# ReLU²-attention followed by an h-swish MLP: the MLP begins at step 30 instead of 33, and the splits of x move with it

## Chip, cores and metric

One Trainium2 chip (trn2), one core. The metric is the device time of one launch in microseconds (us), the median over the runs of a kernel. The engines are PE (TensorE), DVE (VectorE), ACT (ScalarE), POOL (GpSimd) and SP (SyncE, which here only issues DMAs; its queue of issues is written SPq).

## What is computed

```python
scores = (1.0 / S) * np.matmul(z, z.transpose(0, 2, 1))
attn = np.maximum(scores, 0.0) ** 2
x = u * np.matmul(attn, v)                 # (4, 3008, 256)
x = x.reshape(12032, 256)
h = x @ w_in                               # (12032, 2048)
g = h * np.clip(h + 3.0, 0.0, 6.0) / 6.0
y = (g @ w_out).astype(np.float32)         # (12032, 256)
```

## The kernel before

**Precision.** Every operand of a matmul is carried as a high and a low part (names that end in h and l: `ah`/`al`, `vh`/`vl`, `xh`/`xl`, `gh`/`gl`), and a product is three matmuls. To *split* a tensor is to copy it to the high part on ACT and to subtract that copy from it on DVE, which leaves the low part.

**Attention.** A batch (4 of them) has six chunks of 512 query tokens (448 in the last), and a chunk has twelve pairs of key blocks. One **step** g is one pair: 288 steps, 72 per batch, numbered in the order in which they run. In step g the scores of the pair of step g+2 are made (matmuls into the PSUM tiles `s`, relu to `rt` on ACT, squares to `r`, then the high part `ah` on ACT and the low part `al` on DVE), and the products with v of step g's own pair are added up in the PSUM tiles `o`. Scores are symmetric, so a pair that was made before is not made again: its transposed blocks were kept in DRAM (stores `d<-r`, L342 and L356 to L370), are loaded back (`l<-d`, L342, two pairs ahead at most) and transposed on DVE (`rm<-l`, L381, in the program three steps ahead of their use). In a batch's chunk 4 (steps 48 to 59 of the batch) eight of the twelve pairs come from such a mirror and one by half; in chunk 5 (steps 60 to 71) ten do; chunk 0 has nearly none. After a chunk's last pair, u is multiplied into the result on DVE (`times_u`, L560), which makes x in place in the tile `u`.

**MLP.** Two chunks of x make one *part* (12 of them). For a part the 2048 hidden columns are taken in eight **groups** of 256, so there are 96 groups. Group m begins at step `MLP_FROM + 3 m`, and its work is spread over three steps: seven products with `w_in` by a Strassen-like scheme (x's pieces B11 to T4 against the weight's pieces) in two PSUM banks, `m` in the trace, of which c21 is emptied by ACT and y by additions on DVE (L91, into `ra` and `hb`); gates on DVE (L706); the split of g; and in the next three steps the products with `w_out` (`y<-gh`, `y<-gl`). A product into bank y can start only when the addition on DVE has read what was in it: S4·B22, at the start of a group's third step, waits so for the addition of S1·T1 into `hb`. What is left of the groups when attention is over runs alone, in a tail.

**Split of x.** Before a part's first group, `split_x` (L564 on) makes its pieces: nine parts (between `yield`s) of additions and splits, on DVE and ACT. The first three hold the bulk: three subtractions, a copy, then a low part and one more subtraction. For part 0 the table in the step loop gives one of the nine to each of steps 24 to 32; for each later part three to each of three steps, placed by `AFTER`. In the tail the last part's pieces are spread by two per group, and what is left is made at group 87. Behind a part's split stands `load_u` (L549): the load of the next u into the only `u` tile, issued by SP, which has to wait until the split has read the old one.

**Weights.** They come as float64 and are converted, added up and split on DVE in 173 small operations, given out by `build_rate` (L808): four per step from step 18, five from `MLP_FROM`.

**Order.** All of this is written out by hand in the step loop; each engine and each issuing queue runs its instructions in that order.

Of the kernel before, what the change touches and what calls it, by code (L numbers as in the profile page):

```python
# [22 lines left out]
NFP = NF // 2  # L23
NPR = B * NCH // 2

MLP_FROM = 33
EVERY = 3
SPLIT_FROM = 24
AHEAD = 2
# [2 lines left out]
WARM = 10  # L32
AFTER = MLP_FROM - 27

# [5 lines left out]
def relu2_attention_then_hswish_mlp(  # L40
# [74 lines left out]
    def fetch_raw(kind, q):  # L115
        cols = slice(q * 2 * P, q * 2 * P + 2 * P) if kind == "in" else slice(0, D)
        src = w_in if kind == "in" else w_out[q * 2 * P:q * 2 * P + 2 * P]
        src = src.rearrange("(k p) f -> p k f", p=P)
        if now < MLP_FROM - 6:
            raw = opool.tile([P, 2, 2, D], F32R, tag="wo", name="wraw")  # L120
# [163 lines left out]
    def split_z(b, k):  # L284
        zx, zy = zt[b, k]
        raw = raws.pop(("z", k))
        if (b, k) == (0, 0):
            nc.scalar.copy(out=zx[0:64], in_=raw[0:64])
            nc.vector.tensor_copy(out=zy[64:128], in_=raw[64:128])
            sub(zx[64:128], raw[64:128], f(zy[64:128]))  # L290
            sub(zy[0:64], raw[0:64], f(zx[0:64]))
            return
        split(zx[0:64], zy[0:64], raw[0:64], b == 0)
        split(zy[64:128], zx[64:128], raw[64:128], b == 0)
# [254 lines left out]
    def load_u(i):  # L549
        t0, n = tokens(i)  # L550
        t = raw_x[i] = upool.tile([P, 2, 2 * CH], F32, tag="u", name="u")
        nc.sync.dma_start(
            out=t[:, :, :n], in_=ut[:, t0:t0 + n].rearrange("(k p) t -> p k t", p=P)
        )
# [9 lines left out]
    def split_x(i):  # L564


        raw = raw_x[i]
        n = tokens(i)[1] // 2
        left, right = raw[:, :, :n], raw[:, :, n:2 * n]
        new = xt[i] = {}  # L570

        def piece(k, src):
            shape = [P, 2, CH] if k < 3 else [P, CH]
            homes = ((xpool, f"xh{k}"), (xpool, f"xl{k}"))
            if i == NPR - 1:
                homes = ((apool, "ah"), (apool, "al")) if k < 3 else ((zpool, "zx"), (zpool, "zy"))
            xh, xl = (
                pool.tile(shape, F32R, tag=tag, name=f"x{w}{k}")
                for (pool, tag), w in zip(homes, "hl")
            )  # L580
            hi, lo = (x[:, :, :n] if k < 3 else x[:, :n] for x in (xh, xl))
            nc.scalar.copy(out=hi, in_=src)
            for r in range(2 if k < 3 else 1):
                new[2 * k + r] = (hi[:, r], lo[:, r]) if k < 3 else (hi, lo)
            return lambda: sub(lo, src, f(hi))

        if i < NPR - 1:
            pool, tag = (rpool, "r") if i else (hpool, "hb")
            t = pool.tile([P, 2, CH], F32, tag=tag, name="t")[:, :, :n]
        else:  # L590
            t = lpool.tile([P, 16, 64], F32, tag="l", name="t")
            t = t.rearrange("p k f -> p (k f)").rearrange("p (r n) -> p r n", r=2)[:, :, :n]
        sub(t[:, 0], right[:, 1], right[:, 0])
        sub(right[:, 0], right[:, 0], left[:, 0])
        sub(t[:, 1], right[:, 1], right[:, 0])
        yield
        low = piece(0, left)
        yield
        low()
        sub(left[:, 1], left[:, 1], t[:, 1])  # L600
        yield
        low = piece(2, t)
        yield
        low()
        yield
        low = piece(1, right)
        yield
        low()
        yield
        low = piece(3, left[:, 1])  # L610
        yield
        low()
        raw_x.pop(i)
        yield
# [193 lines left out]
    def build_rate(g):  # L808
        return 0 if g < 2 else 2 if g < 4 else 1 if g < 12 else 3 if g < 18 else 4 if g < MLP_FROM else 5

# [17 lines left out]
    def run(it, n=99):  # L828
        for _ in range(n):
            next(it, None)  # L830
# [9 lines left out]
    with tc.manual_schedule():  # L840
# [18 lines left out]
        for i, (b, c) in enumerate(chunks):  # L859
            ahead = b + 1 if c == NCH - 1 and b + 1 < B else None  # L860
            for p in range(NPAIR):
                g = i * NPAIR + p
                pair = pairs[g]
                if i == 0:
# [6 lines left out]
                    if p % 2 == 0 and 0 < p < NPAIR - 4:  # L871
                        split_z(0, p // 2 + 2)
                at_mlp, on = divmod(g - MLP_FROM, EVERY)
                early, now = g < MLP_FROM - 2, g
                if at_mlp < 0:
# [95 lines left out]
                done, since = divmod(g + 1 - AFTER, NFP * EVERY)  # L971
                if g == SPLIT_FROM:
                    xs = split_x(0)
                if SPLIT_FROM <= g < SPLIT_FROM + 9:
                    run(xs, 1)
                if g == SPLIT_FROM + 8:
                    load_u(1)
                if done > 1 and since in range(1, 4):
                    if since == 1:
                        xs = split_x(done - 1)  # L980
# [4 lines left out]
        xs = split_x(NPR - 1)  # L985
        left = range((len(pairs) - MLP_FROM) // EVERY, NPR * NFP)
        units = [
# [95 lines left out]
```

## Time and profile before

| | |
|---|---|
| median of 3 runs | 1832.74 us (1832.39 to 1834.52) |
| the profiled execution's own time | 1833.69 us |
| its span in the trace | 1831.9 us |
| PE busy | 1801.4 us (98%), 8426 matmuls |
| DVE busy | 1505.2 us (82%) |
| ACT busy | 1196.3 us (65%) |
| mean granted PE clock | 0.998 |

PE is busy nearly all the time, so the time follows from how many matmuls there are and from the few places where PE stands still or runs at the lower clock. A share of busy time over the whole span says little of those: they are found by stretch.

### The profile page before, as it was taken

What the parts mean: (1) busy time and instruction counts of PE and PEld (TensorE: products, weight loads), DVE (VectorE), ACT (ScalarE), POOL (GpSimd) and SP (SyncE); (2) the same over time, 40 slices, a digit from 0 to 9 for tenths busy, and PEclk for the clock granted to TensorE, in tenths of its full rate; (3) what the DMA queues carried; (4) which work ended last, traced back from release to release, by engine and by line L of the source; (5) the groups of instructions that cost most, each with busy time, mean ns of one, the idle gap of its engine ahead of it and who ended that gap; (6) DMA issues with size and microseconds to landing.
All of it is one profiled execution on the core that took longest, in us unless ns stands there. A gap on an engine that the chain in (4) does not pass through costs nothing.

```text
span 1831.9 us, 23310 instructions
## 1 busy us (share of the span) xinstructions
PE 1801.4 (98%) x8426; PEld 1584.7 (87%) x8426; DVE 1505.2 (82%) x1767; ACT 1196.3 (65%) x1640; POOL 55.2 (3%) x90
## 2 busy tenths in 40 slices
PE   8999999999999999999999999999999999999999
PEld 7877888988998888888899888888889988888888
DVE  8999988988778788897877877888877787787776
ACT  7896655767656555676766655667675665564565
POOL 1000000100000000010000000001000000000000
PEclk9999999999999999999999999999999999999999
DMA  8868896665664767856665667594565667676343
GB/s 227 242 220 264 212 221 183 188 190 172 183 159 140 193 168 152 229 161 202 186 178 135 177 176 178 130 258 151 160 202 144 173 186 175 143 171 162 109 167 128
DMA packets 440307, 329.50 MB, mean 180 GB/s; under 512 B 278656, under 2 KB 397440, under 8 KB 440192
## 3 DMA queue, kind: packets, MB, share of 16 engines
q1 hardware_dynamic: 432672, 304.16, 60.8%
q0 software_dynamic: 7520, 23.86, 4.5%
q8 instruction: 66, 1.08, 0.3%
q14 instruction: 49, 0.40, 0.1%
HBM read 241.70 MB, written 86.25 MB: 179 GB/s over the span
## 4 chain that ended last, share of the span: by engine, by line
PE 56%; issue 24%; DVE 11%; ACT 4%; DMA 2%; SPq 1%; POOL 0%; DVEq 0%; ACTq 0%; POOLq 0%
PE o L73 22%; PE y L73 16%; PE m L73 14%; PE s L73 5%; DVE al L88 2%; DMA l<-d 1%; DVE rm L381 1%; DVE gl L88 1%; DVE rb L706 1%; ACT gh L766 1%; DVE ra L706 1%; SPq L342 1%; DVE r L462 1%; DVE hb L91 1%; DVE xl L88 0%
## 5 line engine op out<-in xcount | busy, mean ns | idle before, releaser
L73 PE MATMUL m<-xh,wi 128*128 128x512 f32 (+1 forms) x1344 | 476.9, 378 | 8.0 <-DVE hb L91 4.4
L73 PE MATMUL o<-ah,vl 128*128 128x512 f32 (+1 forms) x1152 | 433.2, 376 | 9.8 <-DVE u L560 6.3
L73 PE MATMUL o<-ah,vh 128*128 128x512 f32 (+1 forms) x1152 | 432.0, 375 | 0.0
L73 PE MATMUL y<-gh,wo 128*128 128x512 f32 (+1 forms) x1536 | 388.6, 375 | 0.5 <-ACT gh L766 0.5
L73 PE MATMUL o<-al,vh 128*128 128x512 f32 (+1 forms) x1104 | 328.8, 376 | 2.9 <-DVE al L88 2.9
L73 PEld LDWEIGHTS y<-gh,wo 128*128 128x128 f32 x1536 | 289.9, 189 | 35.8 <-ACT gh L766 1.8
L73 PEld LDWEIGHTS m<-xh,wi 128*128 128x128 f32 x1344 | 254.9, 190 | 48.3 <-DVE hb L91 9.2
L73 PEld LDWEIGHTS o<-ah,vl 128*128 128x128 f32 x1152 | 217.7, 189 | 41.6 <-DVE u L560 8.7
L73 PE MATMUL m<-xl,wi 128*128 128x512 f32 (+1 forms) x672 | 252.4, 376 | 0.0
L73 PEld LDWEIGHTS o<-ah,vh 128*128 128x128 f32 x1152 | 218.0, 189 | 26.6
L73 PEld LDWEIGHTS o<-al,vh 128*128 128x128 f32 x1104 | 208.6, 190 | 30.0 <-DVE al L88 5.4
L73 PE MATMUL y<-gl,wo 128*128 128x512 f32 (+1 forms) x768 | 226.4, 376 | 0.9 <-DVE gl L88 0.5
L441 ACT ACTIVATE rt<-s 128x512 f32<-128x512 f32 (+1 forms) x310 | 180.0, 593 | 71.2 <-PE s L73 64.3
L462 DVE TENSOR_TENSOR r<-rt 128x1024 f32<-128x1024 f32 (+2 forms) x128 | 147.4, 1151 | 81.0 <-ACT rt L441 80.9
L747 ACT ACTIVATE ra<-m,three 128x512 f32<-128x512 f32 (+1 forms) x96 | 65.1, 678 | 174.9 <-PE m L73 132.0
L91 DVE TENSOR_TENSOR hb<-hb,m 128x512 f32<-128x512 f32 (+1 forms) x192 | 128.6, 670 | 59.7 <-PE m L73 59.0
L88 DVE TENSOR_TENSOR al<-r,ah 128x1024 fp32r<-128x1024 f32 (+3 forms) x147 | 164.3, 1118 | 5.7 <-ACT r L460 3.8
L469 ACT ACTIVATE ah<-rt 128x1024 fp32r<-128x1024 f32 (+1 forms) x155 | 163.7, 1056 | 4.9
L73 PEld LDWEIGHTS y<-gl,wo 128*128 128x128 f32 x768 | 144.7, 189 | 20.5 <-DVE gl L88 3.6
L88 DVE TENSOR_TENSOR gl<-rb,gh 128x1024 fp32r<-128x1024 f32 (+2 forms) x97 | 115.2, 1189 | 57.2 <-ACT gh L95 56.7
L381 DVE STREAM_TRANSPOSE rm<-l 128x1024 f32<-128x1024 f32 (+2 forms) x132 | 149.4, 1132 | 8.4 <-DMA l<-d 8.4
L88 DVE TENSOR_TENSOR al<-rm,ah 128x1024 fp32r<-128x1024 f32 (+1 forms) x132 | 155.2, 1176 | 1.3 <-ACT ah L408 0.9
(86 smaller groups left out, 2170.4 us busy)
## 6 DMA issues: line engine op xcount, KB each, us to landing
wi<-dwin SPq DMA_DIRECT2D x96, 896.0 KB, 5.4
d<-r SPq DMA_DIRECT2D x212, 256.0 KB, 3.2
wo<-dwout SPq DMA_DIRECT2D x96, 512.0 KB, 6.1
l<-d SPq DMA_DIRECT2D x304, 128.0 KB, 4.0
l<-d SPq DMA_DIRECT2D x160, 112.0 KB, 4.7
vraw<-in_v_dram POOLq DMA_DIRECT2D x33, 256.0 KB, 4.6
u<-in_ut_dram SPq DMA_DIRECT2D x8, 1024.0 KB, 5.4
out_dram<-y SPq DMA_DIRECT2D x16, 512.0 KB, 5.3
```

What stands on the lines that cost most here:

```text
L73: nc.tensor.matmul(out, lhsT=lhsT, rhs=rhs, start=start, stop=stop, skip_group_check=part)
L88: nc.vector.tensor_tensor(out=out, in0=a, in1=b, op=ALU.subtract)
L91: nc.vector.tensor_tensor(out=out, in0=a, in1=b, op=ALU.add)
L342: nc.sync.dma_start(out=t[32 * q:32 * q + 32, :nk, :], in_=src[:, c0:c0 + 64].rearrange("(k e) f -> e k f", e=32),)
L381: nc.vector.transpose(out=rn[:, :, :n].rearrange("p r (k e) -> p r k e", e=32), in_=t[:, :n // 32].rearrange("p k (r e) -> p r k e", r=2),)
L441: nc.scalar.activation(out=halved(rn[:, r]), in_=unpaired(s[:, :n]), func=AF.Relu, scale=1.0 / S)
L462: nc.vector.tensor_tensor(out=to, in0=of, in1=of, op=ALU.mult)
L469: nc.scalar.activation(out=hn, in_=rn, func=AF.Square)
L706: nc.vector.scalar_tensor_tensor(out=out, in0=out, scalar=6.0, in1=h, op0=ALU.min, op1=ALU.mult)
L747: nc.scalar.activation(out=ra[:, 1], in_=c21, func=AF.Relu, bias=three)
L766: nc.scalar.copy(out=ga[0], in_=ra)
```

## The change

Group m begins at step `30 + 3 m` instead of `33 + 3 m`. `AFTER`, which places the later parts' splits and the loads of u, is `MLP_FROM - 27`, so it becomes 3 instead of 6. Part 0 is split in steps 24 to 29: two of the nine parts in each of the first three, one in each of the others, and `load_u(1)` stands at the end of step 29 instead of 32. The rate of weight operations rises from four to five at step 30, and two switches of buffers (`MLP_FROM - 6`, `MLP_FROM - 2`) come three steps earlier. At the end, ten groups are left for the tail instead of eleven.

```diff
-MLP_FROM = 33
+MLP_FROM = 30
...
                 if g == SPLIT_FROM:
                     xs = split_x(0)
-                if SPLIT_FROM <= g < SPLIT_FROM + 9:
-                    run(xs, 1)
-                if g == SPLIT_FROM + 8:
+                if SPLIT_FROM <= g < SPLIT_FROM + 6:
+                    run(xs, 2 if g < SPLIT_FROM + 3 else 1)
+                if g == SPLIT_FROM + 5:
                     load_u(1)
```

In steps of a batch (0 to 71), the later parts' splits stood at 6 to 8, 30 to 32 and 54 to 56, and now stand at 3 to 5, 27 to 29 and 51 to 53; a load of u stands at the end of the last step of each. Chunks begin at 0, 12, 24, 36, 48 and 60. The instructions themselves, their number and POOL's order stay as they were.

SP's queue in chunk 4 of batch 0 before: the load of the next u stands just ahead of the mirrored blocks of chunk 5's third and fourth pair (`l<-d_959`):

```order
L342 DMA l<-d_1823 32x16x64 x8
L342 DMA l<-d_2249 32x8x64 x4
L238 DMA wi<-dwin 128x1792
L238 DMA wo<-dwout 128x1024
L342 DMA l<-d_552 32x14x64 x8
L552 DMA u<-in_ut_dram 128x2x960
L238 DMA wi<-dwin 128x1792
L238 DMA wo<-dwout 128x1024
L369 DMA d_2515<-r_2837 512x1x128
L370 DMA d_2515<-r_2837 256x1x128
L672 DMA out_dram<-y 128x2x512
L342 DMA l<-d_959 32x14x64 x8
```

The same place now:

```order
L342 DMA l<-d_2328 32x8x64 x4
L552 DMA u<-in_ut_dram 128x2x960
L238 DMA wi<-dwin 128x1792
L238 DMA wo<-dwout 128x1024
L672 DMA out_dram<-y 128x2x512
L342 DMA l<-d_552 32x14x64 x8
L672 DMA out_dram<-y 128x2x512
L238 DMA wi<-dwin 128x1792
L238 DMA wo<-dwout 128x1024
L369 DMA d_2590<-r_2921 512x1x128
L370 DMA d_2590<-r_2921 256x1x128
L342 DMA l<-d_959 32x14x64 x8
```

The load of u and the stores of y now stand ahead of chunk 5's first pair (`l<-d_552`), one group of weights earlier, and no longer in front of `l<-d_959`.

DVE in chunk 4 of batch 1, around step 123 of 288 (step 51 of the batch), before:

```order
L91 TENSOR_TENSOR ra<-ra,m 128x512
L88 TENSOR_TENSOR al<-r_6486,ah 128x1024
L706 SCALAR_TENSOR_TENSOR ra<-ra 128x512
L381 STREAM_TRANSPOSE rm<-l 128x1024
L91 TENSOR_TENSOR hb<-hb,m 128x512
```

Now:

```order
L91 TENSOR_TENSOR ra<-ra,m 128x512
L88 TENSOR_TENSOR al<-r_6561,ah 128x1024
L88 TENSOR_TENSOR t<-u 128x512
L88 TENSOR_TENSOR u<-u 128x512
L88 TENSOR_TENSOR t<-u 128x512
L88 TENSOR_TENSOR xl_6601<-u,xh_6600 128x1024
L88 TENSOR_TENSOR u<-u,t 128x512
L706 SCALAR_TENSOR_TENSOR ra<-ra 128x512
L381 STREAM_TRANSPOSE rm<-l 128x1024
L91 TENSOR_TENSOR hb<-hb,m 128x512
```

The five operations of the split's first part now stand ahead of a full transpose and of the addition `hb<-hb,m`, for which S4·B22 waits. Three steps later, where they stood, the transpose is half as wide.

DVE in chunk 0 of batch 1, around step 75, now (before, the five rows with `u` stood 3 steps later):

```order
L91 TENSOR_TENSOR ra<-ra,m 128x512
L88 TENSOR_TENSOR al<-r_3957,ah 128x1024
L88 TENSOR_TENSOR zy<-zraw,zx 64x512
L88 TENSOR_TENSOR zx<-zraw,zy 64x512
L88 TENSOR_TENSOR t<-u 128x480
L88 TENSOR_TENSOR u<-u 128x480
L88 TENSOR_TENSOR t<-u 128x480
L88 TENSOR_TENSOR xl_3996<-u,xh_3995 128x2x480
L88 TENSOR_TENSOR u<-u,t 128x480
L706 SCALAR_TENSOR_TENSOR ra<-ra 128x512
L462 TENSOR_TENSOR r_4022<-rt 128x8x4x32
L91 TENSOR_TENSOR hb<-hb,m 128x512
```

Here they come right behind the last split of the batch's z (`zy`, `zx`), and a square (`r<-rt`) and the same addition stand behind them.

## Rows read from the trace of the kernel before

**Rows 1.** The page, part 1: busy us, share and instructions of each engine.

```profile
PE 1801.4 (98%) x8426; PEld 1584.7 (87%) x8426; DVE 1505.2 (82%) x1767; ACT 1196.3 (65%) x1640; POOL 55.2 (3%) x90
```

**Rows 2.** Waits of PE from 230 to 1710 us: us in total, times, longest.

```profile
PE o L73 <- DVE u L560: 6.3, 4, 2.2
PE m L73 <- DVE hb L91: 2.2, 3, 0.7
```

**Rows 3.** Timeline of PE, chunk 5's start: start us, us, ... [idle <-releaser].

```profile
305.96 0.52 PE L73 MATMUL o<-ah,vl 128*128 128x448 f32 x1 [2.24 <-DVE u L560]
...
754.78 0.46 PE L73 MATMUL o<-ah,vl 128*128 128x448 f32 x1 [0.86 <-DVE u L560]
...
1202.34 0.46 PE L73 MATMUL o<-ah,vl 128*128 128x448 f32 x1 [1.19 <-DVE u L560]
...
1650.63 0.46 PE L73 MATMUL o<-ah,vl 128*128 128x448 f32 x1 [2.04 <-DVE u L560]
```

**Rows 4.** Windows, steps 60 and 276: length, PE, PEld, DVE, ACT, POOL, PEclk, DMA, GB/s.

```profile
301.77:311.47 9.70, 7.46 (x28) 6.32 (x27) 7.66 (x8) 3.55 (x6) 0.00 (x0) 0.82 0.96 257
1646.64:1656.14 9.50, 7.46 (x28) 6.24 (x27) 7.66 (x8) 3.54 (x6) 0.00 (x0) 0.82 0.98 266
```

**Rows 5.** Timeline of DVE at the first of these places.

```profile
303.09 1.11 DVE L381 STREAM_TRANSPOSE rm<-l 128x896 f32<-128x896 f32 x1 [2.77 <-DMA l<-d]
...
305.23 0.68 DVE L560 TENSOR_TENSOR u<-u,o 128x512 f32<-128x512 f32 x1
```

**Rows 6.** Timeline of SP's issues ahead of it.

```profile
287.59 0.40 SPq L552 DMA_DIRECT2D u<-in_ut_dram  x1
...
293.62 7.89 SPq L342 DMA_DIRECT2D l<-d  x8
```

**Rows 7.** Waits of SP's queue, whole span.

```profile
SPq L552 <- DVE xl L88: 80.2, 10, 8.8
```

**Rows 8.** Timeline of DVE, step 124 (52 of batch 1), no split there.

```profile
704.89 0.68 DVE L706 SCALAR_TENSOR_TENSOR ra<-ra 128x512 f32<-128x512 f32 x1
705.50 1.24 DVE L381 STREAM_TRANSPOSE rm<-l 128x1024 f32<-128x1024 f32 x1
708.40 0.69 DVE L91 TENSOR_TENSOR hb<-hb,m 128x512 f32<-128x512 f32 x1 [1.67 <-PE m L73]
```

**Rows 9.** Timeline of DVE, three steps later: the split's first part begins, and what follows it.

```profile
721.80 0.69 DVE L88 TENSOR_TENSOR t<-u 128x512 f32<-128x512 f32 x1
...
725.72 0.68 DVE L706 SCALAR_TENSOR_TENSOR ra<-ra 128x512 f32<-128x512 f32 x1
```

**Rows 10.** Timeline of PE: T4's last matmul and S4·B22's first, steps 76, 100 and 124.

```profile
409.70 0.59 PE L73 MATMUL m<-xh,wi 128*128 128x512 f32 x2
...
561.62 0.57 PE L73 MATMUL m<-xh,wi 128*128 128x480 f32 x2
...
709.86 0.59 PE L73 MATMUL m<-xh,wi 128*128 128x512 f32 x2
```

**Rows 11.** Timeline of DVE, step 76 (4 of batch 1), behind the split of z.

```profile
405.31 0.69 DVE L706 SCALAR_TENSOR_TENSOR ra<-ra 128x512 f32<-128x512 f32 x1
406.92 1.22 DVE L462 TENSOR_TENSOR r<-rt 128x1024 f32<-128x1024 f32 x1 [0.92 <-ACT rt L441]
408.17 0.69 DVE L91 TENSOR_TENSOR hb<-hb,m 128x512 f32<-128x512 f32 x1
```

**Rows 12.** Timeline: DVE in step 100 (28 of batch 1), PE in step 103 (31).

```profile
555.51 0.66 DVE L706 SCALAR_TENSOR_TENSOR ra<-ra 128x480 f32<-128x480 f32 x1
...
580.48 0.47 PE L73 MATMUL m<-xh,wi 128*128 128x480 f32 x1 [0.74 <-DVE hb L91]
```

**Rows 13.** Windows: steps 24 to 32, 33 to 35, 36 to 47 (columns as in rows 4).

```profile
95.16:131.25 36.09, 33.00 (x146) 26.57 (x144) 35.44 (x54) 34.11 (x49) 2.84 (x4) 1.00 0.67 226
131.25:150.84 19.59, 16.23 (x71) 12.64 (x69) 18.93 (x32) 14.49 (x21) 0.71 (x1) 1.00 0.92 276
150.84:229.47 78.63, 75.93 (x346) 64.42 (x344) 75.90 (x112) 52.98 (x74) 4.27 (x6) 1.00 0.80 224
```

## Prediction

> **What bounds the kernel.** I read the page's busy times first: PE is busy 1801.4 of 1831.9 us [rows 1], 0.214 us for each of 8426 matmuls. The change takes no matmul away, so its effect can only lie in the time that PE loses between them. I took those losses apart by stretch.
>
> From 230 to 1710 us, where attention and MLP run side by side, nearly all of PE's waits have one of two causes [rows 2]. The larger is four waits of 6.3 us together, one per batch, each at the first matmul of chunk 5 [rows 3]. In the first and the last of them the granted clock of the step is 0.82 [rows 4]: behind a standstill of over 2 us PE ran for a while at 1.2 instead of 2.4 GHz. 9.70 x 0.18 = 1.75 us and 9.50 x 0.18 = 1.71 us went that way. With some 0.2 us per place until matmuls follow each other again, the four places cost 6.3 + 3.5 + 0.7 = 10.5 us.
>
> What they wait for: the product with u, which DVE reached late because it stood 2.77 us in front of a transpose whose mirrored block had not landed [rows 5]. DVE runs in order, so everything behind that transpose was late. The block was late because SP issued it at 293.62 us, behind the load of the next u, which went out only at 287.59 us [rows 6]: that load waits for the split to have read the old u, up to 8.8 us with SP's whole queue behind it [rows 7], and then u, two weights, a store and the blocks all go out at once.
>
> The second cause is the 2.2 us of S4·B22 waiting for the addition into `hb` [rows 2], 0.74 us in each of steps 103, 175 and 247 (31 of the batch) [rows 12], right behind the first part of a split of x. Before 230 us the picture is another one: in steps 24 to 32 DVE is busy 35.44 of 36.09 us, in steps 33 to 35 18.93 of 19.59 us [rows 13]. There DVE is the bound, since it also converts the weights. The steps before 24 are the same in both kernels.
>
> **The four waits at chunk 5.** The load of u now goes into SP's queue at step 53 of the batch instead of 56. It will hold the queue as long as before, since the split that it waits for moves with it. But what then stands behind it is chunk 5's first block, which DVE transposes in the program at step 57, three steps or some 18 us later, and not the block that is wanted two steps later. The blocks that were late have only the usual store and weights ahead of them, and the stores of y are three steps earlier. Between the load's issue and theirs SP took 293.62 - 287.59 = 6.0 us for what is now mostly elsewhere [rows 6], and they have to come only 2.77 us earlier [rows 5]. So I price these waits at nothing: **-10.5 us**. Bounds: nothing gained, if another late load takes the place, and 10.5 us.
>
> **The splits in chunk 4 (steps 51 to 53), four times.** Here DVE has room on average, but the order matters. Without a split, in step 124, DVE began the gate at 704.89 us, the transpose at 705.50, and was idle until the addition at 708.40 [rows 8]. The split's first part takes 725.72 - 721.80 = 3.92 us [rows 9], and now stands ahead of the gate: gate at 708.81, transpose at 709.42, addition from 710.58 to 711.18. S4·B22's first matmul is the second of the pair that starts at 709.86 [rows 10], so it was due at 710.07 and now starts some 0.13 us behind the addition, at 711.31. It loses 1.24 us. Three steps later, where the split stood, no such wait of PE is on record [rows 2]: the transpose there is half as wide. 4 x 1.24 = **+5.0 us**. What comes behind (the second and third part of the split) shifts DVE's later work by up to 3 us, but that work is wanted one or two steps later, and there are no scores in these steps that want bank y. Bounds: 0, if DVE runs further ahead than I reckon, and 4 x 3 = 12 us, if the clock falls as in rows 4.
>
> **The splits in chunk 0 (steps 3 to 5), three times.** The same reckoning in step 76: DVE had just finished splitting z, began the gate at 405.31, a square at 406.92, the addition at 408.17 [rows 11]. This split is 480 columns wide, 15/16 of 3.92 = 3.7 us: gate at 409.0, square from 409.6 to 410.85, addition until 411.45. S4·B22 was due at 409.70 + 0.22 = 409.92 [rows 10] and starts at 411.6, 1.66 us late. Where these splits stood before (steps 6 to 8) there is no such wait either [rows 2]. 3 x 1.66 = **+5.0 us**. Bounds 0 and 3 x 3.5 = 10 us, the latter with the lower clock.
>
> **The splits in chunk 2 (steps 27 to 29), three times.** These lose already [rows 12]. In step 100 the gate began at 555.51; with 3.92 us ahead of it, then the gate, a full transpose, a square (1.25 us, as in rows 11) and the addition, this ends near 562.95, and S4·B22 is due at 561.62 + 0.2 [rows 10]: 1.25 us late, where it now loses 0.9 (its 0.74 us of idle time and the restart). 3 x 0.35 = **+1.1 us**. Bounds 0 and 3.
>
> **The start.** This stretch is reckoned by the engine that has more to do. The split of part 0 is 6.9 us of DVE work (3.92, two full low parts of 1.2 and a half one of 0.6, by the tile sizes of rows 8), of which 6.3 lie in steps 24 to 32. So these nine steps have 29.1 us of other work on DVE, 3.25 per step; a step has 16 matmuls, 3.45 us on PE. Before: 35.44 - 31.1 = 4.3 us more on DVE than on PE in steps 24 to 32; 18.93 - 14.9 (69 matmuls) = 4.0 in steps 33 to 35; and 3.9 us lost in steps 36 to 47 (78.63 less 346 matmuls) [rows 13]. Sum 12.2. Now: six steps with the split, 6 x 3.25 + 6.9 = 26.4 against 20.7, 5.7 lost. Then three steps with the first group: 9.75 + 1.8 for three more weight operations (estimated at a half tile's 0.6 us each, as the gate in rows 8) + 4.1 for the group (five half tiles, one full) = 15.65 against 14.9, 0.75 lost. The next three: 18.93 less 0.6 of the split, plus the 2.3 us with which a group ends (two full tiles), 20.6 against 20.1, 0.5 lost; the rest as before. Sum 10.85: **-1.4 us**. PE gets work earlier, DVE's work is only reordered. Bounds: -4, if the first group's own idle time vanishes too, and +3, if ACT, busy 34.11 of 36.09 us there [rows 13], can't take part 0's copies any faster.
>
> **The tail.** One group fewer runs there, which loses nothing by itself. But split_x is given only two groups ahead of group 88 instead of three, so five of the nine parts instead of three come in one go: one full low part (1.2 us) and one copy more ahead of group 87's last addition. The other bank set is in use then; I take **+0.5 us** between 0 and 2.
>
> **Sum.** -10.5 + 5.0 + 5.0 + 1.1 - 1.4 + 0.5 = -0.3 us. The profiled execution took 1833.69 us (span 1831.9 us and what lies around it), so it would take 1833.4; the median of the runs is 1832.74, so I say **1832.4 us**. The smallest difference that this measurement tells from none is about 0.2%, 3.7 us: from 1829.1 to 1836.4 is no change. The large gain is there, and is given back in seven places. This case's own range is 1828.5 to 1836.
>
> **Rivals.**
> 1. *The splits hide* (the gain stays). For it: where the splits of chunks 0 and 4 stood before, DVE absorbed them, since all three waits for `hb` are those of chunk 2 [rows 2]. Against it: the row times above leave the addition 1.2 to 1.7 us late. Time: 1832.4 - 10.0 = 1822.4 us; half hidden, 1827.4.
> 2. *The clock falls at the new waits* (slower). A wait of 2.04 us or more was followed by the lower clock, those of 1.19 and 0.86 us were not [rows 3, 4]. In chunk 0 I reckon 1.66 us. If they come out as long as those two, each costs 1.75 us more and the wait itself 0.4: 3 x 2.15 = 6.5, so 1839 us; if all seven do, 1847. The Trainium skill (TensorE: Matmul & The Clock Gate, "HAM oscillation — how this bites in real kernels") says that a kernel whose PE stands still at every tile pays the return to the lower clock each time; by it, the more places there are the worse, whatever the sum of the waits is. The trace agrees for two of its four places and shows none for the other two.
> 3. *The late block stays late* (slower). The load of u and the stores of y now stand ahead of chunk 5's first block; if that comes late, DVE stands there instead, with the same product with u behind it. It decides if SP's queue is held 10 us longer than the 8.8 us of [rows 7]. 1832.4 + 10.5 = 1843 us.
> 4. *The start gains more*: to its bound of -4, which is 2.6 us more: 1829.8, inside the ranges.
>
> **Chances.** My forecast 0.52 (the fourth is within it), the first rival 0.30 (half of it under 1825), the second 0.11, the third 0.07. Faster by over 0.2% takes the first rival and the forecast's lower edge, 0.28 + 0.04 = 0.32; slower the second and the third and a little of the upper edge, 0.19; the same 0.49. For 8 in 10 the range has to reach to most of the first rival and to the second's lower form: 1823 to 1839 us.
>
> **What would show it.** Right: the row of PE waiting for the product with u is gone or under 1 us, the lower clock with it; the wait for `hb` has risen from 2.2 us with 3 occurrences to about 11 us with 10, at steps 4, 28 and 52 of a batch; DVE is the busier engine until step 29 only, and PE loses some 11 us instead of 12 in steps 24 to 47. Wrong: waits for `hb` that stay at 3 us (the first rival), a granted clock of 0.8 in steps 4 or 52 (the second), a DVE transpose idle behind a load at steps 56 to 60 (the third).

## The result, and the profile after

The changed kernel takes **1843.52 us** in the median of 4 runs (1840.57 to 1846.19), beside 1832.60 us of the kernel before on the same chip: a ratio of **1.0056** (95% interval 1.0042 to 1.0069). I had said 1832.4 us and a range of 1823 to 1839 us. The profiled execution took 1846.19 us, its span is 1844.4 us: 12.5 us longer than the span before. It is the slowest of the four, so what its trace shows as lost can be up to 2.7 us more than the median lost. PE did the same work:

The page, part 1, of the kernel after (columns as in [rows 1]):

```profile
PE 1802.7 (98%) x8426; PEld 1586.2 (86%) x8426; DVE 1504.4 (82%) x1767; ACT 1199.7 (65%) x1640; POOL 55.4 (3%) x90
```

**Where attention and MLP run side by side, the time came out as reckoned.** Waits of PE from 230 to 1710 us, after:

```profile
PE m L73 <- DVE hb L91: 9.4, 10, 1.0
PE s L73 <- DVE hb L91: 1.1, 3, 0.4
PE s L73 <- ACT rt L441: 0.9, 3, 0.3
PE y L73 <- ACT gh L766: 0.8, 1, 0.8
```

Windows of steps 60 and 276, after (columns as in [rows 4]):

```profile
325.32:330.83 5.51, 5.51 (x29) 5.11 (x28) 5.51 (x7) 3.52 (x5) 0.00 (x0) 1.00 0.81 230
1671.71:1677.22 5.51, 5.51 (x29) 5.11 (x28) 5.51 (x7) 3.52 (x5) 0.00 (x0) 1.00 0.86 232
```

The wait for the product with u [rows 2, 3] is gone and the lower clock with it: steps 60 and 276 take 5.51 instead of 9.70 and 9.50 us [rows 4], steps 132 and 204 (6.64 and 6.96 us before) 5.51 too. That is 10.8 us. In exchange the wait for `hb` has grown from 2.2 us in 3 places to 9.4 us in 10.

**The start lost what the rest did not.** Waits of PE from 90 to 230 us, after, the largest two rows:

```profile
PE s L73 <- DVE hb L91: 9.1, 2, 5.9
PE s L73 <- ACT rt L441: 3.5, 4, 1.4
```

Before, the largest row of this stretch is 2.9 us, for `al`. The two waits lie in steps 32 and 44. Timeline of PE there:

```profile
141.91 0.80 PE L73 MATMUL s<-zy,zx 128*128 128x512 f32 x1 [5.87 <-DVE hb L91]
...
226.97 0.80 PE L73 MATMUL s<-zy,zx 128*128 128x512 f32 x1 [3.22 <-DVE hb L91]
```

Windows of these two steps, after:

```profile
134.58:148.78 14.20, 8.33 (x25) 6.50 (x24) 8.09 (x13) 6.39 (x8) 0.00 (x0) 0.76 0.40 143
220.99:233.97 12.98, 9.76 (x31) 7.73 (x30) 8.09 (x13) 6.39 (x8) 0.00 (x0) 0.74 0.50 121
```

The waits are all the idle time of these windows: 14.20 - 8.33 = 5.87 and 12.98 - 9.76 = 3.22 us. The lower clock behind them (windows in the last section) adds 2.9 and 3.1 us. So step 32 loses 8.8 us and step 44 6.3 us.

For the whole stretch I compare windows of steps 24 to 47, first of the kernel before:

```profile
95.16:229.47 134.31, 125.16 (x559) 103.63 (x557) 130.27 (x195) 101.58 (x143) 7.83 (x11) 1.00 0.79 232
```

and of the kernel after:

```profile
94.90:252.32 157.42, 140.29 (x603) 116.46 (x602) 138.53 (x204) 108.06 (x151) 7.84 (x11) 0.96 0.71 212
```

There are 44 more matmuls in it now, since the MLP begins earlier; at 0.214 us each that is 9.4 us of work that later steps need not do. The rest, 157.42 - 134.31 - 9.4 = **13.7 us**, is lost. This difference (window less 134.31, less 0.214 us for each further matmul) is the measure of the start in the experiments below.

**What PE waits for in step 32.** Timeline of DVE there, after:

```profile
133.09 0.69 DVE L91 TENSOR_TENSOR hb<-hb,m 128x512 f32<-128x512 f32 x1
138.63 0.69 DVE L88 TENSOR_TENSOR wl<-t,wh 128x512 fp32r<-128x512 f32 x1 [4.86 <-DMA dwin<-wl]
...
141.18 0.68 DVE L91 TENSOR_TENSOR hb<-hb,m 128x512 f32<-128x512 f32 x1
```

and of ACT:

```profile
137.49 0.62 ACT L111 CAST wh<-t 128x512 fp32r<-128x512 f32 x1 [3.56 <-DMA dwin<-wh]
```

The addition at 141.18 us, which frees the bank for PE, stands behind the write of a weight's low part into `wl`. That write waits until the weight that lay in `wl` has been stored to DRAM (`dwin<-wl`, L209). Until `early` ends, weights rotate over three pairs of tiles (`wh`/`wl`, `gh0`/`gl0`, `gh1`/`gl1`, L214); after that there is one. `early` hangs on `MLP_FROM - 2`, so it now ends at step 28 and not 31. SP's issues at this place, after:

```profile
125.63 0.39 SPq L552 DMA_DIRECT2D u<-in_ut_dram  x1
126.07 0.46 SPq L238 DMA_DIRECT2D wi<-dwin  x1
126.70 0.32 SPq L238 DMA_DIRECT2D wo<-dwout  x1
128.22 1.22 SPq L367 DMA_DIRECT2D d<-r  x2
129.50 1.48 SPq L209 DMA_DIRECT2D dwin<-wh  x1
131.07 0.41 SPq L209 DMA_DIRECT2D dwin<-wl  x1
```

The low part was complete at 126.4 us. Its store went out at 131.07, behind the load of u, two weights and a store of a mirrored block, and the write that waits for it began at 138.63, 7.6 us later. What held SP there was not the load of u, whose issue was over at 126.02 us, but the store `d<-r`: it stores a square that ACT finished only at 127.16 + 1.04 = 128.20 us.

```profile
127.16 1.04 ACT L460 ACTIVATE r<-rt 128x1024 f32<-128x1024 f32 x1
```

In step 44 it is the same pair: issued at 214.42 and 214.84 us, behind `l<-d`, `wi` and `wo`, and awaited by ACT and DVE:

```profile
222.36 0.62 ACT L111 CAST wh<-t 128x512 fp32r<-128x512 f32 x1 [4.35 <-DMA dwin<-wh]
```

```profile
223.69 0.69 DVE L88 TENSOR_TENSOR wl<-t,wh 128x512 fp32r<-128x512 f32 x1 [3.50 <-DMA dwin<-wl]
```

So the theory for the experiments was: the loss is the wait for the store of the only home. Its rivals: A, part 0's split in six steps is too much for DVE; B, the single home alone; and, for the first theory itself, what makes the store late, its place in the queue or its transfer.

### The profile page after: what moved, and what is told of

Read it like the earlier page. It is cut to its first block, busy times and chain, and to the rows that moved or that the text cites. A ratio compares the mean times of both kernels' runs of the same rounds, so it can differ in the third digit from the quotient of the medians.

```text
span 1844.4 us, 23326 instructions
## 1 busy us (share of the span) xinstructions
PE 1802.7 (98%) x8426; PEld 1586.2 (86%) x8426; DVE 1504.4 (82%) x1767; ACT 1199.7 (65%) x1640; POOL 55.4 (3%) x90
## 4 chain that ended last, share of the span: by engine, by line
PE 73%; DVE 13%; issue 8%; DMA 3%; ACT 2%; SPq 1%; POOL 0%; DVEq 0%; POOLq 0%; ACTq 0%
PE o L73 29%; PE y L73 20%; PE m L73 18%; PE s L73 6%; DVE al L88 2%; DVE rm L381 1%; DVE ra L706 1%; DMA dwin<-wl 1%; DVE r L462 1%; DVE hb L91 1%; DMA l<-d 1%; DVE gl L88 1%; DVE xl L88 1%; DMA vraw<-in_v_dram 1%; DVE zx L88 0%
## 5 line engine op out<-in xcount | busy, mean ns | idle before, releaser
L73 PE MATMUL m<-xh,wi 128*128 128x512 f32 (+1 forms) x1344 | 475.9, 377 | 13.7 <-DVE hb L91 9.6
```

Source lines behind the costliest of these rows:

```text
L73: nc.tensor.matmul(out, lhsT=lhsT, rhs=rhs, start=start, stop=stop, skip_group_check=part)
```

## Experiments

Each ratio is against runs of the kernel before on the same chip, with its 95% interval. "After +" is an edit of the changed kernel, "before +" one of the kernel before.

**1. After + the first load of u three steps later**

```diff
-                if g == SPLIT_FROM + 5:
+                if g == SPLIT_FROM + 8:
                     load_u(1)
```

> The changed kernel with load_u(1) three steps later (end of step 32 instead of 29), nothing else. My theory (the time is lost because the only home wh/wl must have been stored before DVE may write it again, and that store was issued at 129.50 and 131.07 us behind and beside the 1 MB load of u and took 7.5 us to land): without u beside it the store lands some 3 to 5 us sooner, the 5.9-us wait of PE at step 32 falls below 3 us with less time at half clock, the one at step 44 (223 us) stays; 1836 to 1840 us. Rival A (the split of part 0 in six steps overloads DVE): the wait stays, 1843 to 1844 us. Rival B (the single home alone): the wait stays, whatever is loaded beside it, 1843 to 1844 us.

Measured: 1838.36 us, 1.0024 (1.0015 to 1.0034). SP's issues, then steps 24 to 47:

```profile
129.73 0.65 SPq L209 DMA_DIRECT2D dwin<-wh  x1
130.47 0.47 SPq L209 DMA_DIRECT2D dwin<-wl  x1
```

```profile
95.21:244.59 149.38, 136.12 (x603) 113.47 (x602) 138.71 (x204) 107.67 (x151) 7.82 (x11) 0.99 0.74 223
```

The stores go out when they did before this edit (130.47 against 131.07 us), since `d<-r` still stands ahead of them (its square is done at 128.45 us), but now neither ACT nor DVE waits for them: ACT writes `wh` at 134.08 us without a pause. What u costs here is the transfer beside it, not its place in the queue. The start's loss falls from 13.7 to 149.38 - 134.31 - 9.4 = 5.7 us; step 44 stays (ACT waits 4.38 us for `dwin<-wh`).

**2. After + the weights' stores on POOL's queue**

```diff
-            nc.sync.dma_start(out=d[:, k], in_=f(t))
+            nc.gpsimd.dma_start(out=d[:, k], in_=f(t))
```

> The changed kernel with the stores of the weight pieces (dwin<-wh, dwin<-wl, dwout<-wh, dwout<-wl) issued from POOL's queue instead of SP's. My theory (SP's queue holds these stores back behind d<-r, wi, wo and the load of u): the first store goes out at 126.5 instead of 129.50 to 131.07 us, the second large one at some 211 instead of 214.84 us; both large waits of PE (5.9 us at step 32, 3.2 us at step 44) fall by about 3 to 4 us, with the half clock behind them gone or shorter; 1832 to 1837 us. If it is the transfer and not the issue: the landing stays at 138.5 us, and so do the waits; 1842 to 1845 us. Rival A (the split): waits stay, 1843 us.

Measured: 1835.48 us, 1.0012 (1.0003 to 1.0021). POOL's issue:

```profile
126.99 0.55 POOL L209 DMA_DIRECT2D dwin<-wl  x1 [3.69 <-DVE wl L88]
```

DVE's wait:

```profile
135.60 0.69 DVE L88 TENSOR_TENSOR wl<-t,wh 128x512 fp32r<-128x512 f32 x1 [2.07 <-DMA dwin<-wl]
```

Steps 24 to 47:

```profile
95.38:241.53 146.15, 135.62 (x603) 113.77 (x602) 138.06 (x204) 107.65 (x151) 18.20 (x31) 0.99 0.72 225
```

The store goes out as soon as its data are there, 4 us sooner, and needs 8.6 us to be done beside the load of u. DVE waits 2.07 us for it instead of 4.86. In step 44 there is no wait for a store left. The start's loss is 146.15 - 134.31 - 9.4 = 2.4 us. Place in the queue and transfer both have their share at step 32; at step 44 the place alone was enough.

**3. After + both edits**

> The changed kernel with both single edits that helped: the stores of the weight pieces on POOL's queue and load_u(1) at the end of step 32. My theory (one cause, the late store of the single home): the edit on the issue leaves 5.0 us lost at step 32, because that store still takes 8.5 us beside the load of u; without u it should land before DVE wants the tile, the loss at step 32 falls below 2 us and nothing else changes: 1831 to 1834 us. Rival A (the split of part 0 has its share): some 4 us stay lost at step 32, 1835 to 1837 us.

Measured: 1835.00 us, 1.0003 (0.9993 to 1.0013). Steps 24 to 47:

```profile
95.84:240.91 145.07, 134.28 (x604) 112.11 (x603) 138.36 (x204) 107.65 (x151) 18.21 (x31) 1.00 0.72 226
```

145.07 - 134.31 - 9.6 = 1.1 us: of the 13.7 us, 12.6 hang on the stores and on what moves beside them. Two edits that only send transfers by another queue or at another time take the change back to no difference. In the median it is little better than the second edit alone (the intervals overlap). It is 1 us above what I expected and at the lower edge of rival A's range; the time does not tell the two apart. The trace does, against A's 4 us lost at step 32 (PE waits 1.70 us for `hb` there), and so does experiment 6.

**4. After + the weights' rate of five from step 33 again**

```diff
-        return 0 if g < 2 else 2 if g < 4 else 1 if g < 12 else 3 if g < 18 else 4 if g < MLP_FROM else 5
+        return 0 if g < 2 else 2 if g < 4 else 1 if g < 12 else 3 if g < 18 else 4 if g < MLP_FROM + 3 else 5
```

> The changed kernel with four weight operations per step until step 32 instead of 29 (five from 33, as in the kernel before). My theory: the write into the single home (the low part of the next weight) falls three operations later on DVE, behind the addition into hb of step 32, and the store has 3 to 6 us more to land; the wait of 5.9 us there falls below 2 us, the one at step 44 moves or goes with the phase of weights against groups: 1830 to 1838 us. Rival (the start loses because DVE has too much to do in steps 30 to 35): the same gain at step 32 but spread, and the weights later late, so 1838 to 1843 us.

Measured: 1835.00 us, 1.0006 (0.9996 to 1.0017). DVE:

```profile
137.11 0.68 DVE L91 TENSOR_TENSOR hb<-hb,m 128x512 f32<-128x512 f32 x1
...
138.82 0.69 DVE L88 TENSOR_TENSOR wl<-t,wh 128x512 fp32r<-128x512 f32 x1 [1.03 <-ACT wh L111]
```

The write into `wl` comes at the same time as in the changed kernel (138.82 against 138.63 us), but the addition into `hb` now stands ahead of it. The store is as late as ever (issued at 130.98 us), and PE waits only 0.79 us for `hb` there. The start's window is 146.20 us with 603 matmuls, 2.5 us lost.

**5. Before + the single home from step 28**

```diff
-                early, now = g < MLP_FROM - 2, g
+                early, now = g < MLP_FROM - 5, g
```

> The kernel before with only the switch to a single home wh/wl three steps earlier (step 28 instead of 31); the MLP begins at 33 as before. Rival B (the single home alone makes the loss): a wait of PE for hb or of DVE for the store of wl of some 5 us appears between 125 and 160 us, 1840 to 1845 us. My theory (it takes the single home together with the load of u ahead of its stores and the first group's additions behind it on DVE): 1832 to 1836 us, at most one or two us lost.

Measured: 1834.02 us, 1.0006 (0.9994 to 1.0019): no difference. ACT waits once for a store, 1.23 us; here SP issues the stores at 126.49 and 127.22 us and the load of u only at 135.64. `early` also decides in which step ACT's deferred copies to high parts are given out (`flush_copies`, L109: a step later once it is over), so this edit and experiment 7 move that too; no run parts the two.

**6. Before + part 0's split in six steps, load of u at step 29**

The diff is the second hunk of the change, alone.

> The kernel before with only the split of part 0 in six steps (24 to 29) and load_u(1) at step 29; the MLP begins at 33. Rival A (the tighter split overloads DVE and is the start's loss): 8 to 13 us more, 1841 to 1846 us. My theory: the load of u here too goes out near 125 us ahead of the stores of a weight, but the pieces still rotate over three homes until step 31 and no group's additions stand behind on DVE; 0 to 3 us more, 1832 to 1837 us.

Measured: 1832.43 us, 0.9991 (0.9980 to 1.0002): no difference, and steps 24 to 47 take 134.58 us with the same 559 matmuls. Rival A is out as a cause by itself: with the MLP at 33, DVE and ACT have room for the split in six steps. In the changed kernel experiment 3 leaves some 1.1 us for it and all the rest.

**7. Before + both of these, the MLP still at 33**

> The kernel before with two parts of the change together: the single home wh/wl from step 28 instead of 31, and part 0 split in steps 24 to 29 with load_u(1) at step 29; the MLP begins at 33 as before. Rival (single home and early load of u are enough for the loss at step 32): DVE waits 3 to 5 us for the store of wl near 135 us and PE 4 us or more, 1840 to 1845 us. My theory (it also takes a group's addition into hb, for which PE waits, standing behind the write of wl on DVE): DVE or ACT may wait for the store, but PE has scores and products two steps ahead and loses under 3 us of it, 1832 to 1837 us.

Measured: 1839.87 us, 1.0043 (1.0027 to 1.0059). ACT at step 32:

```profile
135.88 0.62 ACT L111 CAST wh<-t 128x512 fp32r<-128x512 f32 x1 [5.80 <-DMA dwin<-wh]
```

PE:

```profile
137.04 0.79 PE L73 MATMUL s<-zy,zx 128*128 128x512 f32 x1 [5.76 <-ACT rt L441]
```

Steps 24 to 47:

```profile
95.35:238.11 142.76, 127.89 (x559) 105.76 (x557) 130.22 (x195) 102.04 (x143) 7.82 (x11) 0.98 0.74 219
```

Two edits that make no difference each cost 142.76 - 134.31 = 8.4 us together in the profiled execution (1844.91 us); the medians are 1839.87 - 1833.30 = 6.6 us apart. Here my own expectation fell: I had thought that PE loses little unless a group's addition stands behind on DVE. It lost 5.76 us all the same, by another way: ACT stood 5.80 us in front of the write into `wh`, and the relu of the next scores stood behind that on ACT. So the MLP's earlier start is not needed for the loss at step 32. It takes the single home and, as experiment 1 shows, a large load beside its stores.

**8. After + the later splits as 2, 4, 3 instead of 3, 3, 3**

```diff
-                    run(xs, 3)
+                    run(xs, (2, 4, 3)[since - 1])
```

> The changed kernel with the later parts' split given out as 2, 4 and 3 of its nine parts in its three steps instead of 3, 3 and 3, so that only the three subtractions and a copy (2.1 us of DVE) stand ahead of the addition into hb in the first of them. My reckoning of the steady part: the ten waits for hb of 9.4 us together (230 to 1710 us) fall to three or fewer of under 1 us, with nothing new in their place: 8 to 11 us less, 1833 to 1836 us. If the larger middle portion makes a wait of its own at steps 5, 29 and 53: 1840 to 1844 us. The start (steps 24 to 47) is not touched.

Measured: 1848.05 us, 1.0074 (1.0057 to 1.0091), no gain over the changed kernel, and above both of the ranges that I had given. Waits of PE from 230 to 1710 us:

```profile
PE s L73 <- DVE hb L91: 6.1, 6, 1.7
PE y L73 <- DVE gl L88: 5.9, 7, 0.8
PE y L73 <- ACT gh L766: 1.3, 1, 1.3
```

The ten waits of 9.4 us at S4·B22 are gone, as reckoned; 5.0 us more in front of the scores and 5.9 us in front of the products with `gl` have come in their place, some 4 to 6 us later. My "nothing new in their place" was wrong: the work that I moved held up what DVE does next.

**9. Before + u loaded from POOL's queue**

```diff
-        nc.sync.dma_start(
+        nc.gpsimd.dma_start(
             out=t[:, :, :n], in_=ut[:, t0:t0 + n].rearrange("(k p) t -> p k t", p=P)
         )
```

> The kernel before with the loads of u issued from POOL's queue instead of SP's; the MLP begins at 33 and the splits stay where they were. My theory of the steady part (the four waits at chunk 5 come from SP's queue standing behind the load of u, not from where the split or the MLP stands): the row of PE waiting for the product with u falls from 6.3 us to under 1 us, the lower clock goes with it, the waits for hb stay at 2.2 us with 3 occurrences; 8 to 11 us less, 1822 to 1826 us. Rival: the mirrored blocks are late because the 1 MB of u moves beside them, whoever issues it; then the waits stay, 1831 to 1835 us.

Measured: **1827.73 us, 0.9963** (0.9951 to 0.9976), faster than both kernels, but between the ranges of my theory and of the rival. Waits of PE from 230 to 1710 us:

```profile
PE o L73 <- DVE u L560: 2.7, 3, 1.2
PE m L73 <- DVE hb L91: 2.2, 3, 0.7
PE y L73 <- ACT gh L766: 1.7, 2, 1.5
```

POOL's issue ahead of chunk 5 of batch 0:

```profile
288.18 0.72 POOL L552 DMA_DIRECT2D u<-in_ut_dram  x1 [89.66 <-DVE xl L88]
```

SP's:

```profile
291.16 0.52 SPq L369 DMA_DIRECT2D d<-r  x1
...
293.49 0.39 SPq L672 DMA_DIRECT2D out_dram<-y  x1
293.94 6.21 SPq L342 DMA_DIRECT2D l<-d  x8
```

SP's in the kernel before, for the first two of these:

```profile
290.85 0.53 SPq L369 DMA_DIRECT2D d<-r  x1
...
293.18 0.40 SPq L672 DMA_DIRECT2D out_dram<-y  x1
```

The transpose on DVE:

```profile
301.71 1.11 DVE L381 STREAM_TRANSPOSE rm<-l 128x896 f32<-128x896 f32 x1 [1.07 <-DMA l<-d]
```

u goes out as late as before, since it waits for the same split. What is different is the rest of SP's queue: the two weights go out at 279.13 and 281.30 us instead of 288.08 and 288.59, so they are not in the same burst. The blocks still start at 293.94 us, no earlier than the 293.62 us before [rows 6]: it is the stores of a mirrored block and of y that stand just ahead of them, and these wait for their own data. So the load of u in SP's queue is not why SP issues the blocks late, as my theory and the prediction had it. But SP gets their eight issues off in 6.21 instead of 7.89 us [rows 6], DVE waits 1.07 instead of 2.77 us [rows 5], and the granted clock stays at 1.00. Of the 6.3 us [rows 2] 2.7 are left. Whether u's transfer is in the way of that part, as the rival has it, is not shown: no run takes it away.

The Trainium skill (DMA: Bandwidth & Descriptors, "Issuing engines are not separate DMA queues") says that issuing from several engines saves only the sequencer's time per DMA, usually small beside the transfer. By that rule this edit and the second one would give next to nothing. Here it differs: an issue that waits for data holds what stands behind it, up to 8.8 us [rows 7], and with that gone the weights left some 7 to 9 us earlier and the kernel took 0.4% less.

**10. The same + four weight operations per step until step 35**

> The kernel before with the loads of u on POOL's queue (which gave 0.9963 of before) and four weight operations per step until step 35 instead of 32. There DVE is the busier engine, and steps 33 to 36 lose 6.4 us. If DVE's load is the bound there: 3 operations less of about 0.6 us each in steps 33 to 35 give 1 to 2 us more, 0.995 to 0.996 of before. If the writes of the weights now fall into a worse phase with the groups: a new wait for the store of wl, 0.998 to 1.002 of before.

Measured: 1828.45 us, 0.9976 (0.9965 to 0.9987): not faster than without, and between the two ranges that I had given. Steps 24 to 47 take 133.68 us, 0.4 us less than in experiment 9 (134.13), but the rest to 1826 us takes 0.9 us more (1597.09 against 1596.22 us). A wait for a store is there again: ACT waits 3.0 us for `dwin<-wh`.

## Why the prediction was wrong

By its steps, in its order:

- **The four waits at chunk 5** (said -10.5 us): 10.8 us are gone, and no transpose waits there any more. DVE did stand in front of a transpose whose block was late, as told, and the burst has moved away. But the reason given for the lateness, that SP issued the blocks behind the load of u, holds only in part: without that load in SP's queue they still go out at 293.94 us (experiment 9). In the changed kernel SP issues them 325.32 - 314.30 = 11.0 us ahead of step 60, instead of 301.77 - 293.62 = 8.2. Of these 2.8 us some 1.4 come from the square in front of them, which DVE begins 13.5 instead of 12.1 us ahead of step 60 (311.83 and 289.64 us); the rest I put down to the store of y, which no longer stands there. Their eight issues then take 4.29 instead of 7.89 us. The lower clock was priced somewhat high, since a step's mean also counts idle time: 3.42 x 0.46 = 1.6 us at 305.96 us instead of 1.75. And it is not paid in every execution: in experiment 6 the same wait is 2.19 us long, without the lower clock. That 10.5 and 10.8 us lie so close is in part luck.
- **The splits in chunk 4** (said 1.24 us at each of four places): the row of step 124 has PE waiting 1.04 us, with the restart 1.2. DVE's order is the one I had written down: t at 726.55, the gate at 730.47, 3.92 us apart.
- **The splits in chunk 0** (said 1.66 at each of three): 0.88 us for `hb` and 0.29 for the relu in step 76, with two restarts 1.6. **In chunk 2** (said 0.35 more): 0.88 instead of 0.74 us, less than half of it. All seven new places together: 7.2 us more in the row for `hb`, 0.9 in a new row for the relu and some 0.2 per place for the restart, 9.5 against 11.1 us. The mechanism is right and the sum near; the row for the relu I had not foreseen.
- **The tail** (said +0.5): PE's waits from 1700 us on are 0.8 us longer, within the bounds.
- **The start** (said -1.4, bounds -4 to +3): measured **+13.7 us**. This is the step that failed, and by itself it is more than the whole difference in span. (In it, [rows 13] has 71 matmuls in steps 33 to 35 where I took 69, which moves 0.4 us.)

What failed in it is the sentence "PE gets work earlier, DVE's work is only reordered". I had reckoned the stretch by how much DVE has to do, as if nothing in it waited for a transfer. The change has two edits there that I left without a price, although both were listed: the switch to one pair of weight tiles comes three steps earlier, and the load of u goes into SP's queue at step 29, amid these stores. The first leaves the next weight's write on ACT and DVE no other place to go until the store has landed; the second, by its transfer, makes the writes begin 3.4 to 3.9 us later (137.49 and 138.63 us, against 134.08 and 134.72 in experiment 1). Neither makes a difference alone (experiments 5 and 6), both together cost 8.4 us, 6.6 in the medians (7). The step's own reckoning was not far off, though its sign was: with stores and load out of the way the start loses 1.1 us (3) where I had -1.4, within the bounds, and the kernel takes the time of the kernel before, which is what I had forecast.

Step 44's 6.3 us have the same cause but another way to it, which I read from the order of the issues: the rate of five operations from step 30 and the groups from step 30 bring the write of the next weight just behind `wi`, `wo` and a waiting `l<-d` on SP. The wait goes with the stores' own queue (2) and nearly goes with the old rate (4), where DVE waits 1.20 us for the store.

Of the rivals, the second and third named a loss of this size but at other places: no lower clock appeared at the seven waits (all of 1.04 us or less), and no transpose waits more than 0.3 us for its block. The first, that the splits hide, did not hold either. I had no rival that ends at the start.

What stays open: which of the two edits of experiment 3 carries how much of the last microsecond: the medians differ by 0.5 us from the second alone, the windows of steps 24 to 47 by 1.1 us, both within the intervals. The 2.7 us left in experiment 9 were not taken apart further, nor how its gain divides between the weights' earlier loads and POOL's queue. Single waits for `gh` of 0.7 to 1.7 us come and go between runs that are alike in their steady part (one of 0.8 us after the change, none before, two of 1.9 us together in experiment 6); they are not explained.

## What to carry to other kernels

When a schedule is moved by one constant, list everything that hangs on it, and look at each switch of buffers first: with fewer buffers a write waits for a store, and then the store's place in its issuing queue, and what moves beside it, are on the path of the compute engines. Two edits can be free one by one and cost 7 to 8 us together, so a sum of parts that were each priced alone needs a look at what they share. Before work is moved to dodge a transfer that waits in a queue, try to send that transfer by a queue where nothing urgent stands behind it (POOL's: there only loads of v and z for the next batch): here this took one word and gained 0.4%, where the rearrangement lost 0.6%.

## What was unexpected of the hardware

- A store of 448 KB was done some 7.6 us after its issue beside a load of 1 MB and two weights, and 8.6 us in experiment 2; without that load ACT could write the tile of the store issued at 129.73 us at 134.08, so it took 4.4 us at most. Windows of 126 to 131 us have DMA at a share of 0.86 in the changed kernel and of 0.33 in experiment 1.
- After the waits of 5.87 and 3.22 us PE ran at a granted clock near the lower of its two levels (1.2 GHz) for 6.8 us each, twice as long as after the 2.24 us in the kernel before, where 305.96 to 309.38 us have 0.54. The length of the wait alone does not decide it: in experiment 1 the wait of 3.23 us in step 44 was followed by 3.4 us at the lower clock (221.25 to 224.66 us have 0.50), in experiment 4 one of 1.42 us was too (123.80 to 127.22 us have 0.50), and in experiment 6 one of 2.19 us at 305.97 us was not. So the sign in the prediction's second rival, a wait as long as 2.04 us, does not hold from run to run. Windows behind the two waits, kernel after:

```profile
141.91:148.73 6.82, 6.82 (x18) 5.53 (x19) 4.82 (x8) 4.57 (x6) 0.00 (x0) 0.57 0.12 36
226.97:233.80 6.83, 6.83 (x18) 5.50 (x19) 4.81 (x8) 4.56 (x6) 0.00 (x0) 0.55 0.13 37
```

So each of these two waits cost about 3 us more than its own length: 6.82 x 0.43 = 2.9 and 6.83 x 0.45 = 3.1 us.
